# Early q and k of a windowed attention kernel: two neighbouring tokens of a head in one partition, turned by quarter-array matmuls

## The chip, the cores and the metric

One core of a Trainium2 chip (trn2) runs the whole kernel. The metric is the device time of one execution in microseconds (us). Three executions of the kernel before took 849.04, 849.40 and 850.57 us; their median is 849.4 us. The trace that is read here is that of another, profiled execution.

## The reference

A sliding-window attention (8 batches, 8 heads, 576 tokens, head size 64; a token sees itself and the 63 tokens before it) feeds a feed-forward block with a squared ReLU:

```python
scores = scale * np.matmul(q, k.transpose(0, 1, 3, 2))
rel = pos[:, None] - pos[None, :]
mask = (rel >= 0) & (rel < 64)
scores = np.where(mask, scores, -1000000000.0)
attn = softmax(scores)                       # row maximum taken off, 1e-9 added to the sum
x = np.matmul(attn, v).astype(np.float32)    # -> [8*576 tokens, 8*64]
h = x @ w_in                                 # 512 -> 2048
out = np.maximum(h, 0.0) ** 2 @ w_out        # 2048 -> 512
```

The weights arrive as 64-bit floats and the kernel turns their words into 32-bit values itself.

## The kernel before, in words

The 4608 tokens are worked through in 12 tiles of 384 tokens (six blocks of 64). The first tiles are the start-up: their order of work is written out by hand, as one string of short names (`order`, from line 488), in which every name issues one step on its engine in this order. The later tiles are ordered by a planner with costs and due times (`Plan`, line 640); the change does not touch them.

Each engine works through its own instructions strictly in the order of issue, and all DMAs are issued by one queue, SP's. The names of the string that matter here:

- `L0` to `L4` load q and k of batch 0, 128 tokens at a time (`L4`: 64), and `N0`, `N1` those of the first 192 tokens of batch 1 (`load_first`, line 178; the DMAs are on line 185). Each step issues one DMA for q and one for k. A token lies in one partition, with its 8 heads of 64 values side by side; what the DMA reads at a stretch is one head of one token, 256 bytes. Two such steps share one buffer of the pool `w`.
- `T0` to `T9` and `U0` to `U3` turn what was loaded (`turn_first`, lines 188 to 197): TensorE transposes 128 columns (two heads) at a time, four such transposes of one batch `t` and one `d` (which pairs of heads) into one bank of PSUM, `j` and `i` (q or k) picking the quarter of the bank. `T0`, `T3` and all later ones use bank 5, `T1` and `T2` the banks 6 and 7.
- `t0a`, `t1d` and so on copy a bank to SBUF (`copy_first`, line 199, the copy on line 202); the last letter names the engine, `a` ScalarE and `d` VectorE. A new turn into bank 5 waits for the copy before it. Of batch 0, `t0`, `t4`, `t5`, `t7` and `t8` go to ScalarE and `t1`, `t2`, `t3`, `t6` and `t9` to VectorE; all four of batch 1 go to ScalarE.
- `S` computes the scores of four pairs of blocks (line 235, matmuls of a quarter of the array, 64 by 64), `o` and `s` select them (lines 243, 252, 253), `z`, `y`, `e`, `f`, `k`, `R`, `m` are the softmax (255 to 272), `X` and `x` transpose and mask the weights (276, 280), `V` multiplies them with v (298), `H` and `Q` split the result in two parts (313, 315).
- `w0`, `w1`, ... load a pair of weight blocks, 512 KB each (lines 104 and 105); `a`, `b`, `c`, `d`, `h`, `l` turn the words into two 32-bit parts (lines 118 to 132, on ScalarE and VectorE). `v0`, ... load v (line 157).
- `M`, `r`, `p`, `g`, `G`, `O` are the feed-forward block (lines 404, 413, 416 or 418, 421, 423, 446).
- `K5` and the like are matmuls of the identity with itself into a bank nobody reads, as many as the number says (line 512).

A step with a capital letter of TensorE and the copies behind it are tied to each other by semaphores that the framework sets from the buffers that are read and written. The beginning of the string:

```python
L0 L1 w0 L2 T0 v0 T1 t0a t1d S0 w1 T2 o0a T3 K5 t2d v1 s0 t3d a0 z0 S1 L3 y0 b0 f0 N0 T4 K3 c0 o1a L4
t4a s1 T5 K5 e0 w2 d0 t5a N1 k0 z1 h0 S2 R0 y1 v2 m0d e1 l0 X0 K6 o2a x0 a1 v3 s2 V0 f1 b1 H0a k1 T6 K4
w3 z2 R1 y2 t6d m1p v4 f2 Q0 T7 X1 c1 t7a U0 e2 x1 S3 u0a k2 d1 V1 o3a T8 v5 H1a R2 s3 m2p t8a T9 a2 Q1
X2 t9d z3 h1 U2 K2 w4 b2 y3 u2a U1 K4 f3 w5 x2 u1a w6 c2 U3 e3 S4 w7 l1 u3a V2 k3 o4a v6 R3 H2a s4 m3p
```

Of the kernel before, what the change touches and what calls it, by code (L numbers as in the profile page):

```python
# [8 lines left out]
F32 = mybir.dt.float32  # L9
# [6 lines left out]
P = 128  # L16
QB = 64
# [12 lines left out]
def window_attention_relu2_ffn(ctx: ExitStack, tc: tile.TileContext, q, k, v, w_in, w_out, out):  # L30
    nc = tc.nc
    pe, dve, act, pool, sp = nc.tensor, nc.vector, nc.scalar, nc.gpsimd, nc.sync
    B, H, S, D = q.shape
# [16 lines left out]
    wpool = ctx.enter_context(tc.tile_pool(name="wpool", bufs=NF))  # L50
    wst = ctx.enter_context(tc.tile_pool(name="wst", bufs=1))

    banks = psum.tile([P, 8, DM], F32, name="banks")
# [19 lines left out]
    o_bank = Turn([6, 7])  # L73

    ident = const.tile([P, P], F32, name="ident")
# [84 lines left out]
    def get_turned(b, d):  # L160
        if (b, d) not in turned:
            turned[b, d] = qk_t[:, d]
        return turned[b, d]
# [8 lines left out]
    nats, first = {}, {}  # L172

    def tokens(b, t):
        return min(P, (FIRST if b else S) - t * P)


    def load_first(b, t):
        n = tokens(b, t)
        if t % 2 == 0:  # L180
            both = wpool.tile([P, 2, 2, H * D], F32, name="w")
            for i in range(2):
                nats[b, t + i] = both[:, i]
        for i, x in enumerate((q, k)):
            sp.dma_start(nats[b, t][:n, i].rearrange("s (h d) -> s h d", d=D),  # L185
                         x[b, :, t * P:t * P + n, :].rearrange("h s d -> s h d"))

    def turn_first(b, t, d):
        n = tokens(b, t)
        early = b == 0 and 0 < 2 * t + d < 3  # L190
        ps = banks[:, o_bank() if early else 5].rearrange("p (j i s) -> p j i s", j=2, i=2)
        if b and (t, d) == (0, 0):
            first[b] = wpool.tile([P, 2, 2, 2, FIRST], F32, name="w")
        for j in range(2):
            for i in range(2):
                pe.transpose(ps[:, j, i, :n], nats[b, t][:n, i, (2 * j + d) * P:(2 * j + d + 1) * P], ident[:n, :n])
        return ps

    def copy_first(b, t, d, ps, copy):
        n = tokens(b, t)  # L200
        qk = first[b][:, d] if b else get_turned(b, d)
        copy(qk[:, :, :, t * P:t * P + n].rearrange("p j i s -> p (j i) s"), ps.rearrange("p j i s -> p (j i) s")[:, :, :n])

# [340 lines left out]
    with tc.manual_schedule(engines={E.PE, E.DVE, E.Activation, E.Pool, E.SP}):  # L546
        for token in order.split():
            op, eng = token[0], token[-1] if token[-1] in "dap" else None
            n = int(token[1:].rstrip("dap"))
            if op in "LN":  # L550
                load_first("LN".index(op), n)
            elif op == "v":
                load_v(*divmod(n, (NB + 1) // 2))
            elif op == "w":
                fetch_w(n)
            elif op == "q":
                load_qk(1 + n // NPAIR, n % NPAIR)
            elif op == "D":
                turn(1 + n // NPAIR, n % NPAIR)
            elif op in "TU":  # L560
                ps_f[op, n] = turn_first("TU".index(op), *divmod(n, 2))
            elif op in "tu":
                copy_first("tu".index(op), *divmod(n, 2), ps_f[op.upper(), n], copier(eng))
            elif op == "K":
                idle(n)
            elif op in "abcdhl":
                weight(op, n)
            elif op == "M":
                hs[n] = mm1(*steps[n], lambda kk, part, f=steps[n][1]: wparts[f][:, 0, part, kk * P:(kk + 1) * P])
            elif op in "rpgG":  # L570
                evac(op, n, eng)
            elif op == "B":
                keep(n)
            elif op in "ACEF":
                mix(op, n)
            elif op == "O":
                mm2(*steps[n], *gs.pop(n), lambda part, f=steps[n][1]: wparts[f][:, 1, part])
            elif op in "ZW":
                for tb in range(NTB):
                    put(op, steps[n][0], tb)  # L580
            else:
                section(op, n, eng)
# [448 lines left out]
    for j in range(FULL):  # L1031
        for r in range(2 * SPT):
            i = SPT * NPLAIN + 2 * SPT * (j + 1) + r
            m = 16 * j + (2 * r if r else -4)
            m, n = (0, (1, 4)) if m == 2 else (m, m + 1)
# [60 lines left out]
```

## Time and profile before

| | before |
|---|---|
| median of three executions | 849.4 us (849.04 to 850.57) |
| profiled execution, its own time | 847.38 us |
| span of the profiled execution, first to last instruction | 845.1 us |
| mean granted clock of TensorE in it | 0.998 |
| instructions | 17706 |
| moved by DMA | 173.92 MB, mean 206 GB/s |
| packets | 273012, of them 190497 under 512 bytes |
| the early turns (line 196) | 56 transposes, first start 4.3 us, last 35.7 us |

How to read the profile: PE is TensorE's matmuls, PEld its weight loads (they overlap with matmuls), DVE VectorE, ACT ScalarE, POOL GpSimd, SP the engine that issues the DMAs. A row of the timeline has the start, the duration, the engine, the line of the kernel, the operation, the buffers (out<-in), the shapes and how many were merged, and in brackets the idle time of the engine before it with what ended it. A row of the stretches has the stretch, its length, the busy time of PE, PEld, DVE, ACT and POOL with the number of instructions, the granted clock, the DMA engines' busy share and GB/s. A row of the waits names who waited for whom, how long in all, how often and the longest. Matmuls are pipelined, so durations of single ones overlap, and a share above 1 of the DMA engines means that packets overlap as well.

### The profile page before, as it was taken

What the parts mean: (1) busy time and instruction counts of PE and PEld (TensorE: products, weight loads), DVE (VectorE), ACT (ScalarE), POOL (GpSimd) and SP (SyncE); (2) the same over time, 40 slices, a digit from 0 to 9 for tenths busy, and PEclk for the clock granted to TensorE, in tenths of its full rate; (3) what the DMA queues carried; (4) which work ended last, traced back from release to release, by engine and by line L of the source; (5) the groups of instructions that cost most, each with busy time, mean ns of one, the idle gap of its engine ahead of it and who ended that gap; (6) DMA issues with size and microseconds to landing.
All of it is one profiled execution on the core that took longest, in us unless ns stands there. A gap on an engine that the chain in (4) does not pass through costs nothing.

```text
span 845.1 us, 17706 instructions
## 1 busy us (share of the span) xinstructions
PE 829.0 (98%) x6754; PEld 761.2 (90%) x6754; DVE 590.5 (70%) x889; ACT 407.3 (48%) x1127; POOL 184.9 (22%) x239
## 2 busy tenths in 40 slices
PE   7899999999999999999999999999999999999998
PEld 5788989899999999999999999999999999999997
DVE  5899996746767866767687765788755668544553
ACT  5887874646446555544442354453454424222221
POOL 1220003204557420311320121141112132010110
PEclk9999999999999999999999999999999999999999
DMA  9989956584688875999896797999785556686411
GB/s 230 231 257 346 306 239 130 86 171 126 153 210 251 214 170 119 305 245 238 169 319 225 179 217 161 285 224 271 212 237 157 188 194 182 236 259 212 136 66 74
DMA packets 273012, 173.92 MB, mean 206 GB/s; under 512 B 190497, under 2 KB 239649, under 8 KB 270881
## 3 DMA queue, kind: packets, MB, share of 16 engines
q1 hardware_dynamic: 272928, 172.80, 73.8%
q8 instruction: 53, 0.87, 0.5%
q14 instruction: 31, 0.25, 0.1%
HBM read 138.15 MB, written 34.60 MB: 204 GB/s over the span
## 4 chain that ended last, share of the span: by engine, by line
PE 86%; SPq 5%; DVE 3%; DMA 3%; issue 2%; ACT 1%; POOL 0%; DVEq 0%; ACTq 0%; POOLq 0%
PE banks L993 29%; PE banks L912 26%; PE banks L446 11%; PE banks L404 11%; PE banks L235 3%; PE banks L298 3%; DMA w<-in_moe_w_out_dram 2%; PE banks L276 2%; SPq L147 1%; SPq L185 1%; SPq L157 1%; DVE a L123 1%; DVE a L125 1%; SPq L104 1%; DVE g L423 1%
## 5 line engine op out<-in xcount | busy, mean ns | idle before, releaser
L993 PE MATMUL banks<-w 128*128 128x512 f32 x1152 | 257.5, 380 | 0.0
L993 PEld LDWEIGHTS banks<-w 128*128 128x128 f32 x1152 | 215.7, 189 | 28.4
L404 PE MATMUL banks<-x,w 128*128 128x384 f32 x768 | 137.1, 328 | 1.9 <-ACT r L413 1.4
L446 PE MATMUL banks<-w,g 128*128 128x512 f32 x576 | 136.1, 382 | 0.2
L404 PEld LDWEIGHTS banks<-x,w 128*128 128x128 f32 x768 | 126.6, 189 | 6.1 <-ACT r L413 3.3
L912 PE MATMUL banks<-x,w 128*128 128x384 f32 x768 | 130.3, 326 | 0.0
L938 POOL TENSOR_TENSOR g<-g 128x384 f32<-128x384 f32 x64 | 59.5, 934 | 323.1 <-ACT g L949 308.2
L912 PEld LDWEIGHTS banks<-x,w 128*128 128x128 f32 x768 | 125.6, 189 | 0.0
L446 PEld LDWEIGHTS banks<-w,g 128*128 128x128 f32 x576 | 106.2, 189 | 14.4 <-DVE g L423 1.2
L263 ACT ACTIVATE sel<-sel,nm 128x64 f32<-128x64 f32 x272 | 90.8, 336 | 25.9 <-DVE nm L257 22.8
L912 PE MATMUL banks<-w 128*128 128x384 f32 x576 | 100.7, 329 | 0.0
L1001 DVE TENSOR_TENSOR w<-w,banks 128x512 f32<-128x512 f32 x72 | 49.5, 687 | 69.9 <-PE banks L993 69.9
L912 PEld LDWEIGHTS banks<-w 128*128 128x128 f32 x576 | 93.8, 189 | 1.9
L983 ACT CAST w<-w 128x512 fp32r<-128x512 f32 x48 | 29.8, 620 | 72.9 <-PE banks L993 72.9
L413 ACT ACTIVATE r<-banks 128x384 f32<-128x384 f32 x64 | 31.5, 492 | 66.8 <-PE banks L404 64.6
L983 ACT CAST w<-g 128x512 fp32r<-128x512 f32 x48 | 29.7, 621 | 62.2 <-PE banks L993 58.2
L272 POOL TENSOR_TENSOR sel<-sel,nm 128x512 f32<-128x512 f32 x33 | 36.1, 1095 | 107.3 <-ACT g L949 51.7
L263 ACT ACTIVATION_READ_ACCUMULATOR sel<-sel,nm 128x1 f32 x272 | 51.2, 188 | 0.0
L423 DVE TENSOR_TENSOR g<-r,g 128x384 fp32r<-128x384 f32 x64 | 37.6, 588 | 18.0 <-ACT g L421 9.7
L535 POOL TENSOR_TENSOR a<-w 128x256 f32<-128x256 f32 x28 | 24.9, 906 | 105.3 <-DVE w L132 79.6
L280 DVE TENSOR_TENSOR pt<-banks,masks 128x1024 f32<-128x1024 f32 x33 | 40.3, 1220 | 10.9 <-PE banks L276 10.9
L926 DVE TENSOR_TENSOR w<-banks,r 128x384 f32<-128x384 f32 x64 | 38.5, 601 | 13.3 <-PE banks L912 13.0
(103 smaller groups left out, 990.0 us busy)
## 6 DMA issues: line engine op xcount, KB each, us to landing
w<-mixed SPq DMA_DIRECT2D x128, 256.0 KB, 5.1
w<-kept SPq DMA_DIRECT2D x64, 512.0 KB, 7.2
w<-kept SPq DMA_DIRECT2D x96, 256.0 KB, 5.9
kept<-w SPq DMA_DIRECT2D x16, 1024.0 KB, 7.5
vt<-in_v_dram SPq DMA_DIRECT2D x144, 64.0 KB, 2.9
w<-in_moe_w_in_dram SPq DMA_DIRECT2D x16, 512.0 KB, 7.5
w<-in_moe_w_out_dram SPq DMA_DIRECT2D x16, 512.0 KB, 8.4
raw<-in_q_dram SPq DMA_DIRECT2D x112, 72.0 KB, 3.4
```

Of the source, the lines that this page charges most:

```text
L263: act.activation(sels[i][:, w, hd], sels[i][:, w, hd], AF.Exp, bias=nms[i][:, n], scale=SCALE, accum_out=sums[i][:, n])
L272: (dve if eng == "d" else pool).tensor_tensor(p, p, rs[i][:, :, None].broadcast_to([P, SW * 2, QB]), ALU.mult)
L280: dve.tensor_tensor(pts[i].rearrange("p (w n) q -> p w n q", n=2), ps_t[i][:, :, None, :].broadcast_to([P, SW, 2, P]), masks.rearrange("p ...
L404: pe.matmul(h_ps, lhsT=weights(kk, part), rhs=in_turn(x[xx][:, kk // 2, kk % 2]), start=n == 0, stop=n == 3 * NK - 1)
L423: dve.tensor_tensor(gs[n][1], rg.pop(n), gs[n][0].bitcast(F32), ALU.subtract)
L446: pe.matmul(acc(t, tb), lhsT=gg[:, ts], rhs=in_turn(weights(part)), start=f == 0 and n == 0, stop=f == NF - 1 and n == 2)
L912: pe.matmul(ps[:, :TT], lhsT=w[:, part, kk * P:(kk + 1) * P], rhs=in_turn(x[:, xx, kk]), start=n < 4 and m == 0, stop=m == 5, skip_group_c ...
L926: plan("dve", 0.6, lambda: dve.tensor_tensor(to(), ps, other(), ALU.add), [kps, ko], keys, 0, after)
L938: plan("pool", 0.95, lambda: pool.tensor_tensor(x(), x(), x(), ALU.mult), [], keys)
L983: plan("act", 0.62, lambda: act.copy(high(c), src()), g_keys, [kh], 0, freed("hi") if new else [])
L993: pe.matmul(ps, lhsT=gg[:, m // 2, m % 2], rhs=in_turn(wo_slot(w[m])[:, part]), start=m == 0 and n == 0, stop=m == 3 and n == 2)
L1001: plan("dve", 0.72, lambda: dve.tensor_tensor(by_half(parts(tb)), by_half(parts(tb)), ordered(ps), ALU.add), [key], [kp])
```

## The change

A partition now holds two neighbouring tokens of a head: the DMA reads 512 bytes at a stretch (two tokens of one head lie side by side in DRAM) and writes half as many partitions, partitions 0 to 63 of the buffer for even `t`, 64 to 127 for odd `t`. The four transposes of a batch become 16 matmuls with a 64 by 64 (for `T8`, `T9`, `U2`, `U3` 32 by 32) corner of the identity: for each `j`, `i`, for each of the two tokens `e` of a partition and each of the two heads `hd`. Their results stand in PSUM with all first tokens ahead of all second ones. The copy brings the tokens back into order and is issued in two halves, one for each `j`.

```diff
-            both = wpool.tile([P, 2, 2, H * D], F32, name="w")
+            both = wpool.tile([P, 2, H, 2, D], F32, name="w")
             for i in range(2):
-                nats[b, t + i] = both[:, i]
+                nats[b, t + i] = both[i * QB:(i + 1) * QB]
         for i, x in enumerate((q, k)):
-            sp.dma_start(nats[b, t][:n, i].rearrange("s (h d) -> s h d", d=D),
-                         x[b, :, t * P:t * P + n, :].rearrange("h s d -> s h d"))
+            sp.dma_start(nats[b, t][:n // 2, i].rearrange("s h e d -> s h (e d)"),
+                         x[b, :, t * P:t * P + n, :].rearrange("h (s e) d -> s h (e d)", e=2))
 
     def turn_first(b, t, d):
-        n = tokens(b, t)
+        n = tokens(b, t) // 2
...
-        ps = banks[:, o_bank() if early else 5].rearrange("p (j i s) -> p j i s", j=2, i=2)
+        ps = banks[:, o_bank() if early else 5].rearrange("p (j i e s) -> p j i e s", j=2, i=2, e=2)
...
+        r = slice(t % 2 * QB, t % 2 * QB + n)
         for j in range(2):
             for i in range(2):
-                pe.transpose(ps[:, j, i, :n], nats[b, t][:n, i, (2 * j + d) * P:(2 * j + d + 1) * P], ident[:n, :n])
+                for e in range(2):
+                    for hd in range(2):
+                        pe.matmul(ps[hd * D:(hd + 1) * D, j, i, e, :n], lhsT=nats[b, t][:n, i, 2 * (2 * j + d) + hd, e], rhs=ident[r, r],
+                                  start=True, stop=True)
         return ps
 
     def copy_first(b, t, d, ps, copy):
         n = tokens(b, t)
         qk = first[b][:, d] if b else get_turned(b, d)
-        copy(qk[:, :, :, t * P:t * P + n].rearrange("p j i s -> p (j i) s"), ps.rearrange("p j i s -> p (j i) s")[:, :, :n])
+        for j in range(2):
+            copy(qk[:, j, :, t * P:t * P + n].rearrange("p i (s e) -> p i s e", e=2),
+                 ps[:, j].rearrange("p i e s -> p i s e")[:, :, :n // 2])
```

## The prediction

> **What bounds the kernel now.** I read the page first, then the busy time by stretches, the waits of each engine inside those stretches, and the timeline around the longest waits.
>
> ```profile
> PE 829.0 (98%) x6754; PEld 761.2 (90%) x6754; DVE 590.5 (70%) x889; ACT 407.3 (48%) x1127; POOL 184.9 (22%) x239
> PE   7899999999999999999999999999999999999998
> DVE  5899996746767866767687765788755668544553
> DMA  9989956584688875999896797999785556686411
> ```
> ```profile
> 9.80:59.60 49.80, 44.25 (x635) 38.27 (x634) 47.13 (x65) 42.08 (x137) 11.26 (x17) 0.97 0.94 237
> 66.80:130.00 63.20, 62.95 (x336) 58.23 (x337) 61.63 (x68) 48.55 (x67) 0.00 (x0) 1.00 0.81 283
> 130.00:845.00 715.00, 710.75 (x5710) 655.77 (x5708) 473.91 (x748) 310.16 (x916) 170.89 (x207) 1.00 0.72 195
> ```
> TensorE is the bound of the whole, but not of the stage that the change touches: all loads and turns of the early q and k lie before 37 us. From 66.8 us on TensorE is busy 62.95 of 63.20 us and then 710.75 of 715.00, so whatever moves its arrival there moves the end by as much. Before, between 9.8 and 59.6 us (columns: PE, PEld, DVE, ACT, POOL busy), it is VectorE that is fullest: 47.13 of 49.80 us, the 16 DMA engines beside it at 0.94. The change can therefore pay only by closing what is left open on VectorE's line and on what feeds it:
>
> ```profile
> DVE a L120 <- ACT a L118: 0.8, 1, 0.8
> DVE sel L252 <- ACT sel L243: 0.8, 1, 0.8
> ```
> ```profile
> 22.87 0.52 SPq L105 DMA_DIRECT2D w<-in_moe_w_out_dram  x1
> 30.36 1.12 ACT L118 ACTIVATE a<-w 128x1024 f32<-128x1024 f32 x1 [1.25 <-DMA w<-in_moe_w_out_dram]
> 31.39 1.03 ACT L129 CAST w<-a 128x1024 fp32r<-128x1024 f32 x1
> 31.52 0.69 DVE L120 TENSOR_SCALAR a<-a 128x1024 f32<-128x1024 f32 x1 [0.76 <-ACT a L118]
> 32.74 1.11 PE L196 MATMUL banks<-ident,w 128*128 128x128 f32 x4 [0.32 <-ACT w L202]
> 33.65 1.88 PE L512 MATMUL banks<-ident 128*128 128x128 f32 x8
> ```
> ```profile
> 36.81 0.59 ACT L243 COPY sel<-banks 128x512 f32<-128x512 f32 x1 [0.49 <-PE banks L235]
> 37.43 0.50 DVE L252 COPY_PREDICATED_SCALAR sel<-late,neg 128x256 f32 x1 [0.76 <-ACT sel L243]
> ```
> Two holes of 0.76 us each. The first is a load's: the third pair of weight blocks (w2), issued at 22.87 us, releases ScalarE at 30.36 us after 1.25 us of idling, and that releases VectorE at 31.52 us. The second hangs on the same load by a longer way: ScalarE's next step (L129) follows at 31.39 us, only then comes the copy (L202) that frees bank 5, at 32.74 us TensorE can turn the next batch (U1), eight idle matmuls follow, then U3, the scores, ScalarE's copy at 36.81 us and VectorE at 37.43 us. So the load w2 is the lever.
>
> **The change part by part.**
>
> *The loads.* Ahead of w2 in SP's queue stand L0 to L3 and N0, ten loads of 256 KB, and L4, two of 128 KB: 2.88 MB, now in packets of 256 bytes, afterwards in half as many of 512 (two tokens of a head lie together). Number and order of the issues stay, nothing is moved past another queue, and the only wait that grows is that of the next turn in a bank, which now waits for two copies instead of one (priced below). What the packet size does to the rate:
>
> ```profile
> DMA packets 3914, 0.99 MB, mean 215 GB/s; under 512 B 3914, under 2 KB 3914, under 8 KB 3914
> DMA packets 5713, 1.44 MB, mean 216 GB/s; under 512 B 5709, under 2 KB 5709, under 8 KB 5713
> DMA packets 383, 0.39 MB, mean 329 GB/s; under 512 B 1, under 2 KB 382, under 8 KB 383
> ```
> The first two answers are 1.8 to 6.4 us and 17.2 to 23.9 us, almost all early q and k at 256 bytes: 215 and 216 GB/s. The third is 7.0 to 8.2 us, weights at 1 KB: 329 GB/s. No stretch has 512-byte packets alone, so 216 and 329 are the bounds and I take the middle, 272. The 2.88 MB then take 10.6 us for 13.4: w2 lands up to 2.8 us earlier (bounds 0 and 4.6). It needs only 1.25 us for ScalarE's wait to vanish, which is the case from 2.88 MB / 12.1 us = 238 GB/s on. The last stretch alone, 1.31 MB of L3, N0 and L4, gives 6.1 - 4.8 = 1.3 us of it. One thing speaks against it: the new transfers write 64 partitions, the old ones 128. [...] No row here shows a half-partition stream in large packets, so that is the second rival below.
>
> *The start.*
> ```profile
> 5.32 1.76 PE L196 MATMUL banks<-ident,w 128*128 128x128 f32 x7 [0.62 <-DMA w<-in_k_dram]
> ```
> The first turns wait for the first k. With q and k of L0 (0.52 MB) at 272 instead of 215 GB/s it lands 0.5 us earlier (0 to 0.8). I count 0.3, because the turns behind it get somewhat longer.
>
> *The copies.* Each of the 14 becomes two of half the size (one per j): VectorE has 5 (t1, t2, t3, t6, t9), ScalarE 9.
> ```profile
> 9.86 0.69 DVE L202 COPY qk<-banks 128x512 f32<-128x512 f32 x1 [2.06 <-PE banks L196]
> 10.47 0.49 DVE L252 COPY_PREDICATED_SCALAR sel<-late,neg 128x256 f32 x1
> ```
> ```profile
> 29.74 0.42 DVE L202 COPY qk<-banks 128x256 f32<-128x256 f32 x1 [0.17 <-PE banks L196]
> 30.08 0.68 DVE L255 TENSOR_REDUCE nm<-w 128x8 f32<-128x512 f32 x1
> 32.33 0.36 ACT L202 COPY w<-banks 128x256 f32<-128x256 f32 x1
> 32.59 0.34 ACT L263 ACTIVATE w<-w,nm 128x64 f32<-128x64 f32 x1
> ```
> ```profile
> 16.82 0.57 ACT L202 COPY qk<-banks 128x512 f32<-128x512 f32 x1
> 17.28 1.05 ACT L129 CAST w<-a 128x1024 fp32r<-128x1024 f32 x1
> ```
> Instructions overlap a little, so I price from start to start. On VectorE 512 columns hold the engine 0.61 us and 256 columns 0.34: two halves cost 0.68, 0.07 more, 0.35 us in all; four of the five lie on its full line before 30 us, 0.28. On ScalarE 0.46 against twice 0.26: 0.06 more each, 0.54 in all, of which the copies of U2, U1 and U3, 0.18 us, lie on the way to the second hole. The read is new too: neighbouring outputs now come from PSUM words 64 apart.
> ```profile
> L1001 DVE TENSOR_TENSOR w<-w,banks 128x512 f32<-128x512 f32 x72 | 49.5, 687 | 69.9 <-PE banks L993 69.9
> L202 DVE COPY qk<-banks 128x512 f32<-128x512 f32 x4 | 2.7, 677 | 8.3 <-PE banks L196 8.3
> L202 DVE COPY qk<-banks 128x256 f32<-128x256 f32 x1 | 0.4, 425 | 0.2 <-PE banks L196 0.2
> ```
> The nearest row, L1001, reads every second word (its `ordered` view) in 687 ns where the plain copy takes 677. So I take the stride as free; the upper bound, twice the time per element, is the third rival.
>
> *The turns.* Four full-array transposes become 16 matmuls of a quarter of the array, all of one batch in the same half of the rows.
> ```profile
> 13.19 0.66 PE L196 MATMUL banks<-ident,w 128*128 128x128 f32 x4
> 20.78 0.90 PE L298 MATMUL banks<-pt,vt 64*64 64x128 f32 x32 [0.33 <-DVE pt L280]
> ```
> A batch takes 0.66 us. L298 is the nearest row: 32 quarter matmuls in 0.90 us, which over four quarters is 8 waves, some of them with 128 columns. The new batch uses two quarters, so it too is 8 waves, of 64 columns, if the pair runs together: at most 0.90 us; I take 0.76. If the two would not run together it is 16 waves and at most 1.8. Below 0.66 I see no reason. TensorE idles between the turns, so only U1 and U3 on the way to the second hole count: 2 x 0.1 = 0.2 us.
>
> *The sum.* VectorE reaches L120 with 0.3 us won at the start and 0.28 lost in copies, so unmoved, at 30.76 us; w2 is there, the hole of 0.76 closes. ScalarE starts L118 1.25 us earlier; less 0.18 for copies and 0.2 for turns its copy for L252 is 0.87 us earlier. VectorE could be at L252 0.76 us earlier with its hole of 0.76 in front, so the copy is later and sets it: **0.9 us** earlier. After that the way to 66.8 us is VectorE and TensorE in turn, both full, and neither loses work or gains it. The profiled execution, 847.38 us (845.1 of span and 2.3 around it), would become 846.5. It ran 2.0 us below the median of the three, 849.4; the change is taken off the median: **848.5 us**. A measurement of this kernel can tell about 0.2%, 1.7 us, from no change, so the forecast itself counts as no change.
>
> **The rivals.**
>
> *The clock.* Faster than I say.
> ```profile
> 28.40:31.90 3.50, 2.14 (x18) 1.52 (x17) 2.56 (x5) 2.25 (x4) 1.24 (x2) 1.00 1.00 140
> 31.90:35.30 3.40, 3.08 (x16) 2.75 (x14) 3.37 (x5) 3.40 (x16) 0.00 (x0) 0.51 0.69 183
> ```
> ```profile
> 35.64 0.19 ACT L263 ACTIVATION_READ_ACCUMULATOR w<-w,nm 128x1 f32 x1
> 35.95 0.37 ACT L202 COPY w<-banks 128x256 f32<-128x256 f32 x1
> ```
> From 31.9 to 35.3 us the granted clock is 0.51, right behind a stretch in which TensorE did 2.14 us of work, nearly all of it transposes (of the batches T8, T9, U2 and X). U1 and the eight idle matmuls run in the slow stretch, 32.74 to 35.5 us. If plain matmuls in place of three of these batches hold the clock, U1 takes 0.66 and the eight idle ones about half of 1.88: U3 can start some 0.9 us earlier. ScalarE's exponentials end at 35.83 us, so its copy of U3 gains only 0.12 and the copy behind it, for L252, can start at about 36.2 instead of 36.81: 0.6 of the 0.9 come through. Then the second hole closes as well: 0.9 + 0.6 = 1.5 us, and some 0.4 more if the clock rises one stretch earlier at the start too: 847.5 us. [...]
>
> *The loads gain nothing.* If the transfers into half of the partitions stay at 216 GB/s in spite of the larger packets, w2 lands where it did, both holes stay, VectorE's 0.28 us vanish in the first one, and the 0.38 us of copies and turns push the second: 849.8 us, no change.
>
> *The strided copies.* Slower than before. If reading words 64 apart doubles the time per element, (677 - 425) / 256 = 0.98 ns, VectorE's four copies before 30 us (3 x 512 + 256 columns) cost 1.8 us more, and those of U2, U1 and U3 on ScalarE, 1024 columns at about 0.8 ns, 0.8 us; ScalarE's five earlier ones eat its idle time of 1.25 us. VectorE is then late at L120 by 1.8 - 0.76 = 1.0 us, and L252 by that, the 0.8 and the 0.38: 2.2 us, 851.6 us. It decides from a third of a doubling on, a half copy on VectorE of some 0.51 us instead of 0.425, since there the 0.9 us are used up. For it speaks that no row here has such a stride, against it L1001.
>
> **How the numbers follow.** Forecast 0.42, the clock 0.28, loads without gain 0.17, strided copies 0.10, rest 0.03. The forecast's terms carry about 0.8 us to either side (the load 0 to 4.6, the start 0 to 0.8, turns to 1.8), executions differ by another 0.7, so a tenth of its chance lies beyond 1.7 us; of the clock's, two thirds, as the median may hold more slow stretches than the one profiled. Faster by over 0.2%: 0.04 + 0.19 + 0.05 for terms that add up = 0.28. Slower: the strided copies and a little of the load rival and the rest, 0.13. The same: 0.59. The range runs from the clock rival's 847.5 less 0.9, 846.6, to a strided copy of moderate price, 850.8.
>
> **What would show it.** Right: early q and k at clearly more than 238 GB/s with 512-byte packets; no wait of L118 for w2 and none of L120 for L118; 28 copies of 256 or 128 columns at the durations quoted; 224 matmuls in place of 56, a batch at 0.7 to 0.9 us; TensorE's full stretch beginning about 0.9 us earlier than 66.8. Wrong: a granted clock of 1.00 throughout 28 to 36 us (first rival); q and k at 216 GB/s and L118 still waiting (second); copies over 0.5 us (third); or a batch of turns over 1.2 us.

## The result, and the profile after

| | before | after |
|---|---|---|
| median of four executions each | 849.22 us (848.58 to 850.57) | 858.76 us (858.12 to 858.96) |
| ratio to before, 95% interval | | 1.0109 [1.0091, 1.0126] |
| span of the profiled execution | 845.1 us | 856.7 us |
| mean granted clock in it | 0.998 | 0.992 |
| packets of the DMAs | 273012 | 266870 |
| instructions | 17706 | 18504 |

The kernel became 9.5 us slower (858.76 - 849.22); the forecast was 848.5 us, and its range ended at 850.8. The spans of the two profiled executions differ by 11.6 us, as the one of before was a quick one. Of the executions below, one, of the kernel with full-array matmuls, ran at a mean granted clock of 0.752, took 1093.64 us and is left out of its figures. Lines of `turn_first` and below stand some six lines lower: L196 is now L199, L202 is L207, L252 is L258, L512 is L518.

The page of the kernel after (busy time by engine, then tenths of 40 slices):

```profile
PE 843.5 (98%) x7146; PEld 776.8 (91%) x7146; DVE 591.3 (69%) x894; ACT 408.0 (48%) x1136; POOL 184.8 (22%) x239
PE   7999999999999999999999999999999999999998
DVE  4879998675676776866777765688755658554553
DMA  9889983655679785898897887899874655776421
```

TensorE has 392 instructions more, 7146 - 6754. The forecast said 224 matmuls in place of 56, so 168 more; the difference is the first sign of what it missed. The stretches of the kernel after (length, busy PE, PEld, DVE, ACT, POOL with instructions, granted clock, DMA share, GB/s):

```profile
10.00:20.00 10.00, 10.00 (x172) 9.49 (x172) 6.90 (x13) 4.71 (x16) 0.52 (x1) 1.00 1.19 255
40.00:50.00 10.00, 10.00 (x170) 9.26 (x173) 3.59 (x7) 4.62 (x22) 1.28 (x2) 0.50 0.95 284
78.45:141.65 63.20, 63.05 (x337) 58.37 (x338) 61.71 (x68) 48.44 (x67) 0.00 (x0) 1.00 0.73 250
141.65:856.65 715.00, 710.63 (x5709) 655.62 (x5707) 473.80 (x748) 309.86 (x916) 170.75 (x207) 1.00 0.72 195
37.40:40.80 3.40, 3.40 (x46) 3.11 (x48) 3.37 (x5) 1.81 (x10) 0.61 (x1) 0.50 0.52 138
44.20:47.60 3.40, 3.40 (x71) 3.34 (x73) 0.20 (x1) 0.51 (x3) 1.28 (x2) 0.50 0.91 248
```

The same two stretches of ten microseconds before:

```profile
10.00:20.00 10.00, 8.87 (x116) 8.03 (x115) 9.81 (x15) 7.95 (x30) 1.00 (x3) 1.00 1.02 242
40.00:50.00 10.00, 9.38 (x137) 8.01 (x137) 9.86 (x14) 9.71 (x41) 2.87 (x4) 1.00 1.05 374
```

This is the reading that matters most. Before, VectorE was full there (9.81 and 9.86 of 10 us) and TensorE had holes. After, TensorE is busy without a hole (10.00 and 10.00) and VectorE waits: 6.90 and 3.59. The bound of the start-up has changed engines. The two long stretches, shifted by 11.65 us, are the same as before (63.05 against 62.95 us of TensorE, 710.63 against 710.75), so nothing was lost or won behind the start-up: all 11.65 us arise before about 51 us.

TensorE's timeline after shows where:

```profile
6.14 3.14 PE L199 MATMUL banks<-ident,w 64*64 64x64 f32 x53 [0.52 <-DMA w<-in_k_dram]
9.14 2.02 PE L241 MATMUL banks<-qk 64*64 64x64 f32 x30
10.76 3.82 PE L199 MATMUL banks<-ident,w 64*64 64x64 f32 x64
17.80 1.10 PE L199 MATMUL banks<-ident,w 64*64 64x64 f32 x32
33.59 1.12 PE L199 MATMUL banks<-ident,w 32*64 32x32 f32 x32
37.29 1.92 PE L199 MATMUL banks<-ident,w 32*64 32x32 f32 x32
39.14 1.22 PE L518 MATMUL banks<-ident 128*128 128x128 f32 x4
40.29 1.97 PE L199 MATMUL banks<-ident,w 64*64 64x64 f32 x32
42.19 2.07 PE L518 MATMUL banks<-ident 128*128 128x128 f32 x8
44.20 1.92 PE L199 MATMUL banks<-ident,w 32*64 32x32 f32 x32
46.05 0.70 PE L241 MATMUL banks<-qk 64*64 64x128 f32 x8
```

A batch of turns is 32 records, not 16. It takes 1.10 us at full clock, where four transposes took 0.66 (13.19 us in the prediction), and 1.92 us while the clock is low. The trace of before for the same places:

```profile
8.71 1.97 PE L196 MATMUL banks<-ident,w 128*128 128x128 f32 x8
30.77 0.24 PE L196 MATMUL banks<-ident,w 64*128 64x64 f32 x1 [0.56 <-DVE nm L255]
35.84 0.45 PE L235 MATMUL banks<-qk 64*64 64x128 f32 x8
```

T2 and T3 together took 1.97 us at 8.71 us and take 3.82 us at 10.76 us. U2 began at 30.77 us and begins at 37.29, 6.5 us late. From U2 to the scores behind U3 TensorE needed 35.84 - 30.77 = 5.1 us, with waits in it; now U2, idle matmuls, U1, idle matmuls and U3 follow without a gap and need 46.05 - 37.29 = 8.8 us, 3.7 more. With the scores begun 10.2 us late (46.05 against 35.84), the last 1.4 us of the 11.65 come from the scores and products behind them, which still run at half clock.

What the other engines wait for, from 2 to 52 us (total, times, longest): the first row is of before, the next three of after. Then the second hole on VectorE, and ScalarE's step that needs w2:

```profile
DVE qk L202 <- PE banks L196: 8.4, 3, 6.2
DVE qk L207 <- PE banks L199: 11.5, 3, 8.5
DVE sel L258 <- ACT sel L249: 3.4, 1, 3.4
ACT a L118 <- DMA w<-in_moe_w_out_dram: 0.9, 2, 0.5
```
```profile
48.29 0.50 DVE L258 COPY_PREDICATED_SCALAR sel<-late,neg 128x256 f32 x1 [3.38 <-ACT sel L249]
35.60 1.13 ACT L118 ACTIVATE a<-w 128x1024 f32<-128x1024 f32 x1 [0.42 <-DMA w<-in_moe_w_out_dram]
```

The hole ahead of L252, 0.76 us at 37.43 us before, is now one of 3.38 us at 48.29 us. VectorE's longest wait for the turns, 6.2 us before and 8.5 after, is that for the first of them. The wait for the load w2 (ScalarE's L118) has shrunk, to 0.42 us, but not because w2 came earlier: it released L118 at 30.36 us before and releases it at 35.60 us after, 5.2 us later, though it was issued only 1.3 us later (24.15 against 22.87). The wait is short because ScalarE itself is free some 6 us later (35.18 against 29.11). The DMA engines in two stretches of the kernel after that hold almost only early q and k, 2.6 to 7.2 us and 19.6 to 26 us:

```profile
DMA packets 1936, 0.97 MB, mean 211 GB/s; under 512 B 52, under 2 KB 1936, under 8 KB 1936
DMA packets 2368, 1.18 MB, mean 184 GB/s; under 512 B 148, under 2 KB 2365, under 8 KB 2367
```

The packets are twice as large and the rate is no higher: 211 and 184 GB/s where it was 215 and 216.

### The profile page after: what moved, and what is told of

It reads as the page before. It is cut to its first block, busy times and chain, and to the rows that moved or that the text cites. A ratio compares the mean times of both kernels' runs of the same rounds, so it can differ in the third digit from the quotient of the medians.

```text
span 856.7 us, 18504 instructions
## 1 busy us (share of the span) xinstructions
PE 843.5 (98%) x7146; PEld 776.8 (91%) x7146; DVE 591.3 (69%) x894; ACT 408.0 (48%) x1136; POOL 184.8 (22%) x239
## 2 busy tenths in 40 slices
DMA packets 266870, 173.97 MB, mean 203 GB/s; under 512 B 178208, under 2 KB 233504, under 8 KB 264736
## 4 chain that ended last, share of the span: by engine, by line
PE 90%; DMA 3%; DVE 2%; ACT 2%; issue 1%; SPq 1%; POOL 0%; ACTq 0%; POOLq 0%
PE banks L999 29%; PE banks L918 26%; PE banks L452 13%; PE banks L410 13%; PE banks L241 4%; PE banks L304 3%; DMA w<-in_moe_w_out_dram 3%; PE banks L282 2%; DVE a L123 1%; PE banks L199 1%; SPq L185 1%; ACT a L118 1%; ACT r L419 0%; PE banks L518 0%; DVE g L429 0%
## 5 line engine op out<-in xcount | busy, mean ns | idle before, releaser
L286 DVE TENSOR_TENSOR pt<-banks,masks 128x1024 f32<-128x1024 f32 x33 | 40.3, 1220 | 11.0 <-PE banks L282 10.9
L541 POOL TENSOR_TENSOR a<-w 128x256 f32<-128x256 f32 x28 | 24.9, 906 | 105.2 <-DVE w L132 79.5
L937 DVE SCALAR_TENSOR_TENSOR w<-w 128x384 f32<-128x384 f32 x64 | 46.4, 724 | 1.8
```

The costliest lines, as they stand in the source:

```text
L286: dve.tensor_tensor(pts[i].rearrange("p (w n) q -> p w n q", n=2), ps_t[i][:, :, None, :].broadcast_to([P, SW, 2, P]), masks.rearrange("p ...
L937: plan("dve", 0.57, lambda: dve.scalar_tensor_tensor(x(), x(), 0.0, x(), ALU.max, ALU.mult), [], keys)
```

## The experiments

The theory after the result: the turns' matmuls cost TensorE twice what was counted, TensorE becomes the bound, and the low clock doubles that. The rivals: the slower loads alone do it; the loss is the clock's alone; the turns' narrow tiles do it, not their number of passes. A mean granted clock stands beside many results: 0.992 means, by half-clock stretches in an execution of 857 us, some 13.7 us at half clock, which is the stretch of 37.2 to 50.9 us. It does not count the start: there the column shows 1.00 between 10 and 20 us, though the row at 10.76 us takes double time (3.82 us for two batches, where one takes 1.10 at 17.80 us). What is called the low clock at the start is read from such durations alone.

### Full-array matmuls in place of the transposes

Old loads and copies; only the kind of instruction changes.

```diff
-                pe.transpose(ps[:, j, i, :n], nats[b, t][:n, i, (2 * j + d) * P:(2 * j + d + 1) * P], ident[:n, :n])
+                pe.matmul(ps[:, j, i, :n], lhsT=nats[b, t][:n, i, (2 * j + d) * P:(2 * j + d + 1) * P], rhs=ident[:n, :n],
+                          start=True, stop=True)
```

> The kernel before with nothing changed but that the four transposes of a batch are plain matmuls of the full array with the identity. Theory TensorE: 8 records a batch, about 0.9 to 1.0 us instead of 0.66; the array is used in full, so the clock is granted as before or earlier: 850 to 852.5 us. If plain matmuls as such, whatever their size, keep the clock low: 856 us or more with a granted clock of 0.50 after 35 us. Theory loads: as before, 848.5 to 850 us.

Measured: 852.54 us (849.36 to 854.58) against 848.94, ratio 1.0034 [1.0017, 1.0052]. Its timeline:

```profile
9.95 2.05 PE L196 MATMUL banks<-ident,w 128*128 128x128 f32 x16
14.08 1.16 PE L196 MATMUL banks<-ident,w 128*128 128x128 f32 x8
38.01 0.45 PE L236 MATMUL banks<-qk 64*64 64x128 f32 x8
```

The batch is four matmuls in the code and eight records here, 1.16 us at full clock. So in these traces a plain float32 matmul is two instructions (eight records for four), and a transpose is one (four for four, in the row of before at 13.19 us). Four full-array matmuls, 1.16 us, and sixteen quarter ones, 1.10 us, cost the same: what raises the price of a batch at full clock, 0.66 us with transposes, is the two passes (one for each of the two instructions), not the quarter tiles. But that price alone is only a part of the loss: 3.6 us by the medians. The three executions here at a mean granted clock of 1.00, the profiled one among them, took 849.36 to 849.57 us; the median of the kernel before at 0.999 and more is 847.1 us (seven of the 62 executions that ran beside the experiments), so at full clock the dearer batches cost some 2.3 us. Two batches in a row take 2.05 us here at 9.95 us, at full clock already, and 3.82 us in the change.

### The turns alone

Old loads and old copies; the edit is against the kernel before. Each batch is turned by 16 quarter matmuls that read one half of its rows twice and leave out the other half, so half of the tokens are missing.

```diff
+        m = n // 2
+        r = slice(t % 2 * m, t % 2 * m + m)
         for j in range(2):
             for i in range(2):
-                pe.transpose(ps[:, j, i, :n], nats[b, t][:n, i, (2 * j + d) * P:(2 * j + d + 1) * P], ident[:n, :n])
+                for e in range(2):
+                    for hd in range(2):
+                        c = (2 * (2 * j + d) + hd) * D
+                        pe.matmul(ps[hd * D:(hd + 1) * D, j, i, e * m:(e + 1) * m], lhsT=nats[b, t][r, i, c:c + D],
+                                  rhs=ident[r, r], start=True, stop=True)
```

> The turn alone: loads (256-byte packets, 128 partitions) and copies (one a batch) of before, each batch turned by 16 plain quarter matmuls in one half of the rows, as in the change. They read one half of the tokens twice and leave out the other half, so the turned q and k are not the reference's; number, size and place of the matmuls are those of the change. Theory TensorE (the turns are the loss): 855 to 858 us, 32 records a batch, 1.1 us each at full clock and 1.9 at half. Theory loads: 849 to 851 us.

Measured: 857.34 us (856.90 to 857.57) against 848.57, ratio 1.0099 [1.0084, 1.0114]. Two stretches and three rows of its timeline:

```profile
10.00:20.00 10.00, 10.00 (x160) 9.47 (x154) 6.54 (x10) 4.68 (x15) 0.53 (x1) 1.00 0.97 227
41.80:45.20 3.40, 3.40 (x49) 3.11 (x52) 0.59 (x2) 1.37 (x8) 1.28 (x2) 0.50 1.03 360
```
```profile
10.09 3.63 PE L201 MATMUL banks<-ident,w 64*64 64x64 f32 x64
17.82 1.10 PE L201 MATMUL banks<-ident,w 64*64 64x64 f32 x32
44.62 0.70 PE L241 MATMUL banks<-qk 64*64 64x128 f32 x8
```

With q and k loaded as before, 8.8 of the 9.5 us are there, with the same full TensorE, the low clock until 17.8 us by the durations and again at 41.8 us. The turns alone suffice.

How they do it shows beside the full-array matmuls, whose batches cost the same at full clock and whose first k came at the same time. There the batch T4 begins at 14.08 us, here at 17.82, 3.7 us later; the scores behind U3 begin at 38.01 us there and at 44.62 here, 6.6 us later. A batch costs the same at full clock and the loads are the same, so what is left to differ is the time at low clock. By the medians full-array matmuls lost 3.6 us and quarter ones 8.8. So the rival of the narrow tiles is half right: the two passes make the batch dearer, but the larger part of the loss comes with the quarter tiles, by a low clock that lasts longer at the start (by the durations to 17.8 us here and to 8.6 there) and comes again behind 38 us (0.50 here, where the profiled execution of the full-array matmuls has a mean of 1.00).

### The loads alone

The change with eight transposes a batch (64 rows, 128 columns) for the 16 matmuls; rows stand in another order.

```diff
-                    for hd in range(2):
-                        pe.matmul(ps[hd * D:(hd + 1) * D, j, i, e, :n], lhsT=nats[b, t][:n, i, 2 * (2 * j + d) + hd, e], rhs=ident[r, r],
-                                  start=True, stop=True)
+                    h = 2 * (2 * j + d) + e
+                    pe.transpose(ps[:, j, i, e, :n], nats[b, t][:n, i, h].rearrange("s e d -> s (e d)"), ident[r, r])
```

> Loads and copies alone: those of the change, but each batch turned by 8 transposes of 64 partitions by 128 columns in place of the 16 quarter matmuls (32 by 128 where the batch is short). A transpose takes both tokens of one head instead of one token of both heads, so the turned rows stand in another order than the reference's. Theory TensorE: 849.5 to 852 us, early q and k at about 205 GB/s all the same. Theory loads: 855 to 858 us.

Measured: 855.38 us (852.44 to 856.62) against 848.57, ratio 1.0070 [1.0043, 1.0098]. Its timeline around the fourth load, and the stretch behind it:

```profile
23.45 0.34 PE L199 MATMUL banks<-ident,w 64*128 64x64 f32 x2 [0.61 <-DMA w<-in_q_dram]
24.86 0.90 PE L199 MATMUL banks<-ident,w 64*128 64x64 f32 x6 [1.08 <-DMA w<-in_k_dram]
```
```profile
24.90:28.30 3.40, 3.40 (x20) 3.06 (x21) 2.48 (x4) 1.31 (x8) 0.85 (x1) 0.50 1.15 242
```

With cheap turns TensorE reaches T6 early enough to wait for q and k of L3, 0.61 and 1.08 us, and from 24.9 us on the clock is at half. So this half of the change costs by itself too, a good part of it through the clock, as the single executions suggest: three executions at 0.988 to 0.990 took 855.3 to 856.6 us, the one at 0.995 852.44. The two halves of the change lose 8.8 and 6.8 us alone and 9.5 together; they do not add up, probably because with the slow turns TensorE comes late anyway: in the change it reaches T6 at 25.84 us and does not wait for L3.

### Larger transfers over all partitions

The change, but one DMA brings two batches: 512 bytes to 128 partitions.

```diff
-        for i, x in enumerate((q, k)):
-            sp.dma_start(nats[b, t][:n // 2, i].rearrange("s h e d -> s h (e d)"),
-                         x[b, :, t * P:t * P + n, :].rearrange("h (s e) d -> s h (e d)", e=2))
+            m = min(2 * P, (FIRST if b else S) - t * P)
+            for i, x in enumerate((q, k)):
+                sp.dma_start(both[:m // 2, i].rearrange("s h e d -> s h (e d)"),
+                             x[b, :, t * P:t * P + m, :].rearrange("h (s e) d -> s h (e d)", e=2))
```

> The change, but one DMA brings two batches of 128 tokens, so that 512-byte packets go to 128 partitions (96 for batch 1) instead of 64 at a time; half as many DMAs, the first ones twice as large. If it is the half of the partitions that holds the early loads at 205 GB/s: 260 GB/s and more while early q and k run, packets near 30 ns instead of 50. If 512-byte packets are slow for another reason: 200 to 220 GB/s as in the change. Theory TensorE: 856 to 860 us in either case, the turns being unchanged and the first k no earlier. Theory loads: below 855 us if the rate rises.

Measured: 860.03 us (858.37 to 862.26) against 848.57, ratio 1.0133 [1.0109, 1.0156]. Its DMA between 2.9 and 5.0 us, almost all early q and k:

```profile
DMA packets 1359, 0.69 MB, mean 327 GB/s; under 512 B 16, under 2 KB 1359, under 8 KB 1359
```

The same packets run at 327 GB/s when they go to all partitions (345 up to 4.3 us, 292 behind it), and at 184 to 211 when they go to half. So 512-byte packets are not slow as such: it is the half partitions that held the rate, or the size of the DMA, which doubles with the partitions and was not varied alone. It brings no time, since TensorE's turns set the pace and the first k, now twice as large a transfer, releases TensorE only at 6.92 us.

### Both causes taken away

The paired loads of the last experiment with the eight transposes of the one before it: both diffs are shown above, and rows stand in another order.

```diff
+            m = min(2 * P, (FIRST if b else S) - t * P)
...
+                    pe.transpose(ps[:, j, i, e, :n], nats[b, t][:n, i, h].rearrange("s e d -> s (e d)"), ident[r, r])
```

> Both suspected causes taken away at once: 512-byte packets to all partitions (one DMA for two batches) and 8 transposes a batch instead of 16 quarter matmuls; the copies stay those of the change. As in the run with the transposes alone, the turned rows stand in another order than the reference's. If half-partition loads and two-pass quarter matmuls are the whole of the loss: 847.5 to 850.5 us, loads at about 300 GB/s, batches of 0.7 us. If something else of the change (the split copies, the 8 narrow transposes, the clock) carries weight of its own: 852 us or more.

Measured: 851.88 us (847.73 to 854.43) against 848.76, ratio 1.0022 [1.0000, 1.0045], so the loss is gone but for some 3 us, just short of the 852 us from which something else was to carry weight. Those 3 us are also part of the 6.8 us of the loads alone, which had the same transposes and copies; some 3.7 us of the 6.8 are then the half-partition loads' (an estimate, 6.8 - 3.1). The ten executions fall into two groups: three at a mean granted clock of 0.999 took 847.73 to 847.87 us, seven at 0.994 or 0.995 took 851.8 us and more. The profiled one is of the second group:

```profile
31.00:34.40 3.40, 2.81 (x31) 2.38 (x32) 2.82 (x7) 3.23 (x7) 1.38 (x2) 1.00 0.91 264
34.40:37.80 3.40, 3.40 (x20) 2.96 (x18) 3.37 (x5) 3.29 (x19) 0.27 (x1) 0.50 0.84 206
```

A stretch with TensorE at 2.81 of 3.40 us is followed by one at half clock, as at 31.9 us before. The four executions of the kernel before on this chip with a clock of 0.999 or more took 846.57 to 847.66 us. So even at the high clock the paired loads with transposes gain nothing: all three stand behind all four.

### More idle matmuls: the clock taken out

The change with ten more idle matmuls in the weak stretch.

```diff
-  ... T8 v5 H1a R2 s3 m2p t8a T9 a2 Q1 X2 t9d ...
+  ... T8 K4 v5 H1a R2 s3 m2p t8a T9 K2 a2 Q1 X2 K4 t9d ...
```

> The changed kernel with ten more idle matmuls of the full array, four behind T8, two behind T9, four behind X2. If the loss after 35 us is the clock, which full-array work holds up: granted clock 1.00 after 37.4 us (or the slow stretch much shorter than 13.7 us) and 853 to 856 us. If the clock is only a companion and the turns themselves are the loss: 859 to 861 us, the ten matmuls being added to the path.

Measured: 857.28 us (856.08 to 857.75) against 848.94, ratio 1.0096 [1.0074, 1.0118]. That lies between the two expected ranges. All four executions have a mean granted clock of 1.00. The start, and a stretch that ran at half clock in the change:

```profile
10.00:20.00 10.00, 10.00 (x157) 9.36 (x152) 5.96 (x13) 3.68 (x11) 0.52 (x1) 1.00 1.19 262
40.80:44.20 3.40, 3.40 (x74) 3.05 (x73) 3.37 (x5) 1.89 (x11) 0.34 (x1) 1.00 0.95 277
```

The late half-clock stretch is gone and only 1.5 us with it. The ten idle matmuls fill 1.16 + 0.71 + 1.06 = 2.9 us of a line that has hardly a hole. In the profiled execution, the slowest of the four, the low clock at the start also lasted longer, to 19.4 us by the durations where it was 16.8 in the change, and T5 begins at 21.09 us instead of 19.70. Without the ten an execution at full clock would take some 854.4 us (an estimate, 857.28 - 2.9). Against the 847.1 us of the kernel before at that clock, some 7 us by this estimate do not come from the late clock (854.4 - 847.1): they are the two passes, the low clock at the start, which this edit does not touch and the column does not show, and the loads. Some 4 us of the change's time are the late clock's (858.8 - 854.4), of which the kernel before pays 2 as well (849.2 - 847.1). The same idle matmuls in the kernel with paired loads and transposes:

```diff
-  ... T8 v5 H1a R2 s3 m2p t8a T9 a2 Q1 X2 t9d ...
+  ... T8 K4 v5 H1a R2 s3 m2p t8a T9 K2 a2 Q1 X2 K4 t9d ...
```

> Paired loads (one DMA for two batches, 512 bytes to 128 partitions) with transposes, rows in another order, and 10 idle matmuls more (K4 behind T8, K2 behind T9, K4 behind X2). With the paired loads and transposes alone, three executions with granted clock 0.999 took 847.7 to 847.9 us and seven with 0.994 about 851.9. If the slow stretch is all that separates the two groups, and the idle matmuls remove it as they did for the change, nearly all executions take 847.5 to 848.5 us, 0.1% under the kernel before. If the idle matmuls themselves cost (3 us of filler in a stretch that is not TensorE's), or the stretch only marks an earlier delay, it is 850 to 852 us with or without the slow stretch.

Measured: 850.34 us (849.81 to 853.31) against 849.18, ratio 1.0015 [1.0007, 1.0024]. All twelve executions ran at 0.997 or more, and none took the 847.8 us of its quick siblings: the filler costs 2.3 us (850.1 at full clock) where the slow stretch costs 4.

A group of six idle matmuls ahead of the first turn was tried on top of the change's ten:

```diff
-  L0 L1 w0 L2 T0 ...
+  L0 L1 w0 L2 K6 T0 ...
```

> The change with the ten later idle matmuls of the earlier run and six more ahead of T0, so that the clock is full from about 8 us to the end. If the low clock carries most of the loss: 849 to 852 us. If the turns and the loads carry it at full clock too: 853.5 to 856.5 us (857.3 without the early six).

Measured: 857.59 us (856.20 to 861.07) against 848.76, ratio 1.0103 [1.0069, 1.0136]. That is slower than both expected ranges. In the profiled execution, the slowest of the four, the durations are short only from 20.4 us on, later than the 16.8 us of the change, so there the early filler did not bring the clock up; the execution at 1.00 took 856.20 us.

### Fewer idle matmuls in the change

```diff
-  ... w1 T2 o0a T3 K5 t2d ... N0 T4 K3 c0 ... s1 T5 K5 e0 ...
+  ... w1 T2 o0a T3 t2d ... N0 T4 c0 ... s1 T5 e0 ...
```

> The change with its first three groups of idle matmuls left out (K5 behind T3, K3 behind T4, K5 behind T5: 13 matmuls, 26 records; in the change's timeline the runs L518 at 14.51 us, 2.44 us at half clock, at 18.84 us, 0.94 us, and at 20.78 us, 1.38 us). If TensorE is what the start-up after the change runs by, these 4.8 us of filler lie on the path: VectorE's steps at 24 us come 2 to 4 us earlier than in the change, and the time falls to about 855 to 857 us, unless the clock rises later than at 16.9 us or falls for longer than 13.7 us; that would give back up to as much. If TensorE's fullness is only filler that fits between its waits, and the copies or the loads set the pace, VectorE's steps at 24 us stay within 0.5 us of the change and the time stays at 858 to 859 us.

Measured: 859.61 us (858.95 to 859.93) against 849.18, ratio 1.0119 [1.0106, 1.0132]. Its timeline:

```profile
16.47 1.97 PE L199 MATMUL banks<-ident,w 64*64 64x64 f32 x32
19.38 1.86 PE L199 MATMUL banks<-ident,w 64*64 64x64 f32 x29 [0.94 <-ACT qk L207]
26.31 1.10 PE L199 MATMUL banks<-ident,w 64*64 64x64 f32 x32
```

Without the filler T4 and T5 start earlier (16.47 us instead of 17.80 the first), but they run at double time: the durations become short only at 24 us, in place of 17. VectorE's step L286 that begins at 23.82 us in the change begins at 24.30 us here. What the 13 idle matmuls took is given back by the clock, and the run does not say whether filler is on the path. It shows that without these idle matmuls the clock came up 7 us later in the profiled execution.

### The kernel before with other idle matmuls

Two attempts to make the kernel before itself quicker: K3 behind T8 and behind X2, and K6 ahead of T0.

```diff
-  ... T8 v5 H1a R2 s3 m2p t8a T9 a2 Q1 X2 t9d ...
+  ... T8 K3 v5 H1a R2 s3 m2p t8a T9 a2 Q1 X2 K3 t9d ...
```

> The kernel before with six more idle matmuls of the full array in the gaps in front of the slow stretch, three behind T8 and three behind X2 (the clock's price alone, without the turns). If full-array matmuls hold the clock: granted clock 1.00 after 31.9 us in nearly every execution and 0.5 to 1.5 us less than before, 847.5 to 848.7 us. If they do not, or the stretch is covered: 849 to 850 us.

Measured: 850.11 us (848.99 to 852.72) against 848.57, ratio 1.0024 [1.0011, 1.0036]. The profiled execution has a clock of 1.00, so the slow stretch is gone, but two turns wait for k:

```profile
13.92 0.55 PE L196 MATMUL banks<-ident,w 128*128 128x128 f32 x3 [0.87 <-DMA w<-in_k_dram]
23.20 0.55 PE L196 MATMUL banks<-ident,w 128*128 128x128 f32 x3 [0.87 <-DMA w<-in_k_dram]
```

The second, in a kernel of its own:

```diff
-  L0 L1 w0 L2 T0 ...
+  L0 L1 w0 L2 K6 T0 ...
```

> The kernel before with six idle matmuls (12 records, 2.6 us at half clock) ahead of T0, while TensorE waits for the first load. If work in that wait raises the clock one stretch earlier: full clock from about 8 us instead of 11.5, and 846.5 to 848.5 us if TensorE's early turns are on the path, 848.5 to 849.5 us if the loads or VectorE cover it.

Measured: 850.60 us (848.90 to 853.58) against 848.76, ratio 1.0025 [1.0009, 1.0041], with waits of 0.89 and 0.88 us for k and half clock from 23.9 to 27.3 us and 34.1 to 37.5 us. In the first of the two kernels both waits lie ahead of the first added matmul, behind T8, so there they do not come from the edit; in the second the added matmuls stand ahead of both, and this run can't tell. Why these loads land later in some executions is not settled. Neither version beats the kernel before, and both medians lie above what was expected, the first by 0.1 us.

## Why the prediction was wrong, and where it was right

**The step that failed: the turns.** The prediction took the new batch as "16 matmuls" in "8 waves, of 64 columns", 0.76 us. A plain float32 matmul leaves two records in these traces, so the batch is 32 records in 16 waves: 1.10 us at full clock and 1.92 at half. The row that was quoted for it had the answer: L298 shows x32 for one `V`, which the code writes as 16 matmuls, and the row of L512 at 33.65 us shows x8 for the four idle matmuls of `K4`. Read as "32 quarter matmuls in 0.90 us" it gave half the price. The pairs do run together (58 ns a pair of 64 columns at full clock, where 128 columns of a full-array transpose take 109); the upper case of the prediction, "16 waves and at most 1.8", came true for another reason than the one named there. The sum counted 0.2 us for all turns; alone they cost 8.8 us (857.34 us). Only some 2.3 us of this is the price of the passes at full clock, as the full-array matmuls showed; the rest goes with the low clock, for which the sum had no term on this side.

**The conclusion from it: "TensorE idles between the turns, so only U1 and U3 count".** With 0.66 us a batch that was so. With 1.10 and 1.9 us the holes close: TensorE is busy 10.00 of the 10 us from 10 to 20 us, where it was 8.87, and what a turn takes more delays all that follows on TensorE.

**The start: 0.3 us earlier.** The first turns on k start at 6.14 us instead of 5.32, so the first k came 0.8 us later, and the turns that begin there (the rest of T0 and T1), in the low clock, take 3.14 us where they took 1.76. VectorE's L120 of the first weights stands at 15.90 us where it was at 12.38.

**The loads: 272 GB/s, and w2 up to 2.8 us earlier.** Measured 211 and 184 GB/s, and w2 5.2 us later. The late w2 is not what sets the pace: with the turns alone and the old loads L118 begins at 34.99 us without waiting for w2, 0.6 us earlier than in the change. What the second rival supposed of the rate came about, and it was given 0.17: the larger packets gained nothing in half of the partitions (211 and 184 GB/s against 215 and 216), and ran at 327 GB/s in the larger transfers to all of them. Whether the half of the partitions or the smaller DMA held the rate was not shown. The rival's price, 849.8 us, is what failed: it took the rate to stay, and it fell from 216 to 184 GB/s for L3 and what follows. The run with these loads and cheap turns lost 6.8 us, some 3.7 of it, by the estimate above, through the loads to half of the partitions in place of the paired ones: TensorE waited 0.61 and 1.08 us for L3 and the clock was at 0.50 behind the wait.

**The copies: right.** The forms of 256 columns on VectorE and ScalarE after:

```profile
L207 DVE COPY qk<-banks 128x256 f32<-128x256 f32 x8 | 3.0, 414 | 11.5 <-PE banks L199 11.5
L207 ACT COPY qk<-banks 128x256 f32<-128x256 f32 x8 | 2.6, 375 | 6.2 <-PE banks L199 6.2
```

414 ns against 425 in the row of before, although every second output comes from 64 words away (375 ns against 377 on ScalarE): the stride is free here, and the third rival, the only one that was to be clearly slower, is refuted. The slower time came from a term that had no rival on that side: a batch of turns above 1.2 us was named only as a sign that the prediction would be wrong.

**The clock: the opposite of the first rival.** It supposed that plain matmuls in place of the transposes hold the clock. Full-array ones did come to the short durations early (16 records in 2.05 us at 9.95 us). Quarter ones did not: TensorE was busy 3.40 of 3.40 us between 44.2 and 47.6 us and the granted clock stayed at 0.50, and with the change the half clock went from 3.4 us to 13.7. That the kind of instruction decides was the author's supposition and was not shown; over all profiles the line runs elsewhere. By the durations the full clock began between 8.6 and 11.5 us in the four kernels whose turns fill the array, be they transposes or matmuls (the kernel before, its two versions with other idle matmuls, and the full-array matmuls), and between 14.6 and 24.2 us in the nine whose turns fill a part of it, quarter matmuls and 64-row transposes alike (14.6 us with the transposes of the loads alone). That is one execution each, and a correlation; a later first k does not explain it, since with the turns alone and the old loads it was 17.8 us. What these runs show is that the clock does not go with the busy time in the records (in the change TensorE was busy without a hole from 20.30 to 23.75 us at 1.00 and from 44.20 to 47.60 at 0.50); what it does follow stays open.

**The way to the end: right.** Everything behind 51 us is shifted by one amount, and the arrival of the start-up sets the end.

## What to carry to other kernels

Count instructions, not matmuls as the code writes them: look in the trace for a row of the same kind and compare its count with the code, since a plain float32 matmul here is two records and a transpose one (eight and four for a batch of four). In a start-up where one engine is full and the next is at 89%, ask what each added microsecond does to the second engine before asking what the first gains. Larger packets that go to half of the partitions may gain nothing (here 211 and 184 GB/s against 215 and 216), and a price on TensorE is to be worked out at full and at half clock (1.10 and 1.92 us a batch here). Two forms of a matmul that cost the same at full clock can still leave the clock low for different times, as the full-array and the quarter matmuls did here (1.16 and 1.10 us a batch, short durations from 8.6 and 17.8 us on, 3.6 and 8.8 us lost): in a start-up, count that too.

## What the runs showed of the hardware

- A pair of quarter matmuls on the two column halves takes 58 ns of start-to-start time at full clock and 107 at half (the change, the batches at 17.80 and 40.29 us); a full-array transpose of 128 columns takes 109 and 213 (the kernel before, 13.19 and 32.74 us, the second at a granted clock of 0.50).
- The stretch at half clock lasted 3.41 us before (31.95 to 35.36 us) and 13.65 us after (37.24 to 50.90), four times as much. At the start two batches took 3.82 us (the change, 10.76 us) where one took 1.10 at 17.80, while the granted-clock column shows 1.00; that this is a low clock too is the author's reading of the durations.
- A 512-byte packet took about 50 ns of its DMA engine when 64 partitions were written (the change, 19.6 to 26 us: 117.3% of 16 engines' 6.4 us over 2367 packets), and 28 to 33 ns with 128 and DMAs of twice the size (the paired loads, 2.9 to 5.0 us, an estimate: 16 engines at 116.5% and 345 or 292 GB/s).
- A plain float32 matmul left two records, a transpose one: 1.16 us for the eight records of four full-array matmuls, 0.66 for four transposes of the same data.
- Ten idle matmuls behind T8, T9 and X2 removed the half-clock stretch in the change (a mean granted clock of 1.00 in all four executions, 0.992 to 0.994 without them) and in the kernel with paired loads and transposes (0.997 to 1.00 in all twelve, 0.994 or 0.995 in seven of ten without them), and brought 1.5 us at the most.
